# Re-staging a fused sliding-window attention and SwiGLU kernel: token pairs per partition, loads and casts one tile ahead, denominators by exp(-ln), one SiLU function

## The chip, the cores and the metric

The kernel runs on one core of one Trainium2 chip. The metric is the device time of one execution in microseconds (us), and a kernel is quoted by the median of its runs. An execution that is over 1.5% above the fastest of its kernel counts as slow and is left out of the ratios.

Engine names are those of the profile: PE is TensorE (matmul), PEld its weight load, DVE is VectorE, ACT is ScalarE, POOL is GpSimd and SP is SyncE. SPq, ACTq and POOLq are the sequencers of those engines, here mostly issuing DMA transfers. "L217" is line 217 of the kernel that was profiled.

## The reference

Attention over 8 batches, 8 heads, 576 positions and head size 64, in which each query sees only itself and the 63 positions before it; the result, 4608 tokens of width 512, goes through a SwiGLU block of width 1536.

```python
def _attn_ref(q, k, v):                       # [8, 8, 576, 64] each, float32
    scores = 1.0 / np.sqrt(64) * np.matmul(q, k.transpose(0, 1, 3, 2))
    rel = pos[:, None] - pos[None, :]
    mask = (rel >= 0) & (rel < 64)
    scores = np.where(mask, scores, -1e9)
    attn = softmax(scores)                     # [cut: written out in numpy]
    return np.matmul(attn, v)

def _moe_ref(x, w_gate, w_val, w_out):        # [4608, 512], [512, 1536] x2, [1536, 512]
    g = x @ w_gate
    silu = g * (1.0 / (1.0 + np.exp(-g)))
    val = x @ w_val
    return silu * val @ w_out
```

## The kernel before

The 4608 tokens are cut into nine tiles of 512. A tile's attention is done in four units, one for each pair of heads. A unit's parts are: load q, k and v; cast them to bf16 on GpSimd; transpose q and k on TensorE; copy k into a block-diagonal tile `kbd` (two heads share 128 rows); scores; exp; mask; products with v; and division by the row sum. The row sum comes from a matmul with a block of ones, so that it already stands in every row that needs it.

```python
    def transposes(u):                  # [cut: eight transposes into one PSUM tile tp]
        nc.scalar.copy(qT[:], tp[:, 0, :])
        kt = tp[:, 1, :].rearrange("r (j x) -> r j x", x=64)
        nc.vector.tensor_copy(kb[0:64, p, :, 0:64], kt[0:64])
        nc.vector.tensor_copy(kb[64:128, p, :, 64:128], kt[64:128])

    def scores(u):                      # [cut: per half, score matmuls into s_ps]
            nc.scalar.activation(Ef[...], s_ps[...], AF.Exp, scale=0.125)
            nc.gpsimd.tensor_mul(Ef[...], Ef[...], mask[...])

    def products(u):                    # [cut: E times v into o_ps]
        for c in range(2):
            nc.tensor.matmul(d_ps[:], bones[:], E[:, :, c, :], start=(c == 0), stop=(c == 1))
        r = att.tile([P, 512], FP32, name="r", tag="r")
        nc.vector.reciprocal(r[:], d_ps[:])
        nc.vector.tensor_mul(xT[t][:, p, :], o_ps[:], r[:])

    def gate_value(t, m):               # [cut: four gate and four value matmuls]
        nc.scalar.activation(th[:], g_ps[:], AF.Tanh, scale=0.5)
        nc.vector.scalar_tensor_tensor(sg[:], th[:], 1.0, g_ps[:], ALU.add, ALU.mult)
        nc.vector.tensor_mul(hT[t][:, m, :], sg[:], v_ps[:])
```

In the steady part each unit of attention is woven between three of the feed-forward block's twelve gate/value groups and one of the four output projections of the tile before:

```python
        gate_value(t, 3 * s)
        products(w + 4)
        gate_value(t, 3 * s + 1)
        transposes(w + 5)
        project(t - 1, s, ps_o, "o")
        load(w + 8)                     # up to 20 DMA issues on SyncE
        casts(w + 6)
        scores(w + 5)
        gate_value(t, 3 * s + 2)
```

Weights are loaded as float32 and cast by VectorE.

The softmax here doesn't subtract the row's maximum and nothing guards it: scores larger than these inputs give would overflow.

Of the kernel before, what the change touches and what calls it, by code (L numbers as in the profile page):

```python
# [17 lines left out]
def kernel(  # L18
# [10 lines left out]





# [4 lines left out]
    NU = NT * 4  # L38
# [3 lines left out]
    stage = ctx.enter_context(tc.tile_pool(name="stage", bufs=4))  # L42
    wst = ctx.enter_context(tc.tile_pool(name="wst", bufs=4))
    cast = ctx.enter_context(tc.tile_pool(name="cast", bufs=2))
    att = ctx.enter_context(tc.tile_pool(name="att", bufs=3))
    xpool = ctx.enter_context(tc.tile_pool(name="xpool", bufs=3))
    fsb = ctx.enter_context(tc.tile_pool(name="fsb", bufs=3))
    hpool = ctx.enter_context(tc.tile_pool(name="hpool", bufs=2))
    ps_a = ctx.enter_context(tc.tile_pool(name="ps_a", bufs=3, space=PSUM))
    ps_f = ctx.enter_context(tc.tile_pool(name="ps_f", bufs=2, space=PSUM))  # L50
    ps_o = ctx.enter_context(tc.tile_pool(name="ps_o", bufs=1, space=PSUM))
# [5 lines left out]
    vbd = [cst.tile([P, 4, 8, P], BF16, name=f"vbd{i}") for i in range(2)]  # L57
    identb = cst.tile([P, P], BF16, name="identb")
    bones = cst.tile([P, P], BF16, name="bones")
    mask = cst.tile([P, 8, 2, 64], BF16, name="mask")  # L60
# [13 lines left out]
    def load(u):  # L74
        t, p = divmod(u, 4)
        q_f = stage.tile([P, 4, 2, D], FP32, name="q_f", tag="q_f")
        k_f = stage.tile([P, 4, 2, D], FP32, name="k_f", tag="k_f")
        v_f = stage.tile([P, 8, D], FP32, name="v_f", tag="v_f")
        for dst, src in ((q_f, q), (k_f, k)):
            for off, b, s0, n in segments(t):  # L80
                o, s, left = off, s0, n
                while left:
                    if o % P or left < P:
                        m, r = 64, 64
                    else:
                        m, r = left // P * P, P
                    for a in range(2):
                        nc.sync.dma_start(  # L88
                            dst[o % P:o % P + r, o // P:o // P + max(1, m // P), a, :],
                            src[b, 2 * p + a, s:s + m].rearrange("(c r) d -> r c d", r=r),  # L90
                        )
                    o, s, left = o + m, s + m, left - m
        for off, b, s0, n in segments(t):
            for a in range(2):
                nc.sync.dma_start(
                    v_f[64 * a:64 * a + 64, off // 64:(off + n) // 64],
                    v[b, 2 * p + a, s0:s0 + n].rearrange("(j r) d -> r j d", r=64),
                )
        staged[u] = (q_f, k_f, v_f)
# [3 lines left out]
    def casts(u):  # L103
        t, p = divmod(u, 4)
        q_f, k_f, v_f = staged.pop(u)
        q_b = cast.tile([P, 4, P], BF16, name="q_b", tag="q_b")
        k_b = cast.tile([P, 4, P], BF16, name="k_b", tag="k_b")
        nc.gpsimd.tensor_copy(q_b[:], q_f[:].rearrange("r c h d -> r c (h d)"))  # L108
        nc.gpsimd.tensor_copy(k_b[:], k_f[:].rearrange("r c h d -> r c (h d)"))  # L109
        vb = vbd[t % 2]  # L110
        nc.gpsimd.tensor_copy(vb[0:64, p, :, 0:64], v_f[0:64])
        nc.gpsimd.tensor_copy(vb[64:128, p, :, 64:128], v_f[64:128])
        ready[u] = (q_b, k_b)

    raw = {}

    def weights_gv(s):
        for i, src in enumerate((moe_w_gate, moe_w_val)):
            w_f = wst.tile([P, 4, 384], FP32, name="w_f", tag="w_f")
            nc.sync.dma_start(  # L120
                w_f[:], src[:, 384 * s:384 * s + 384].rearrange("(c r) f -> r c f", r=P)
            )
            raw[i, s] = w_f

    def casts_gv(s):
        for i, dst in enumerate((wg, wv)):
            nc.vector.tensor_copy(dst[:, :, 384 * s:384 * s + 384], raw.pop((i, s))[:])

    def weights_o(s):
        w_f = wst.tile([P, 3, DM], FP32, name="wo_f", tag="w_f")  # L130
        nc.sync.dma_start(
            w_f[:], moe_w_out[384 * s:384 * s + 384].rearrange("(c r) f -> r c f", r=P)
        )
        raw[2, s] = w_f

    def casts_o(s):
        nc.vector.tensor_scalar_mul(wo[:, 3 * s:3 * s + 3, :], raw.pop((2, s))[:], 0.5)
# [3 lines left out]
    def transposes(u):  # L141
        t, p = divmod(u, 4)
        q_b, k_b = ready.pop(u)
        tp = ps_a.tile([P, 2, 512], BF16, name="tp", tag="a")
        for i, x in enumerate((q_b, k_b)):
            for c in range(4):
                nc.tensor.transpose(tp[:, i, P * c:P * c + P], x[:, c, :], identb[:])  # L147
        qT = att.tile([P, 512], BF16, name="qT", tag="qT")
        nc.scalar.copy(qT[:], tp[:, 0, :])  # L149
        kb = kbd[t % 2]  # L150
        kt = tp[:, 1, :].rearrange("r (j x) -> r j x", x=64)
        nc.vector.tensor_copy(kb[0:64, p, :, 0:64], kt[0:64])  # L152
        nc.vector.tensor_copy(kb[64:128, p, :, 64:128], kt[64:128])  # L153
        queries[u] = qT
# [3 lines left out]
    def scores(u):  # L158
        t, p = divmod(u, 4)
        qT = queries.pop(u)  # L160
        E = att.tile([P, 8, 2, 64], BF16, name="E", tag="E")
        Ef = E[:].rearrange("r m c x -> r (m c x)")
        for h in range(2):
            s_ps = ps_a.tile([P, 512], FP32, name="s_ps", tag="a")
            lo = 0
            if u < 4 and h == 0:
                lo = 64
            else:
                j = 4 * h - 1
                kb = kbd[t % 2][:, p, j, :] if j > 0 else kbd[(t - 1) % 2][:, p, 7, :]  # L170
                nc.tensor.matmul(s_ps[:, 0:64], kb, qT[:, 256 * h:256 * h + 64])
            for i in range(4):
# [4 lines left out]
                    kbd[t % 2][:, p, j, :],  # L177
# [5 lines left out]
            nc.gpsimd.tensor_mul(  # L183
                Ef[:, 512 * h + lo:512 * h + 512],
                Ef[:, 512 * h + lo:512 * h + 512],
                mask[:].rearrange("r m c x -> r (m c x)")[:, lo:512],
            )
            if t < 8 and t // 4 == h:
                nc.gpsimd.memset(E[:, t, 0, :], 0.0)
        weights[u] = E  # L190

    xT = {}

    def products(u):
        t, p = divmod(u, 4)
        E = weights.pop(u)
        Ef = E[:].rearrange("r m c x -> r (m c x)")
        if p == 0:
            xT[t] = xpool.tile([P, 4, 512], BF16, name="xT", tag="xT")
        o_ps = ps_a.tile([P, 512], FP32, name="ao_ps", tag="a")  # L200
        first = True
        for j in range(-1, 8):
            if j < 0 and t == 0:
                continue
            vb = vbd[t % 2][:, p, j, :] if j >= 0 else vbd[(t - 1) % 2][:, p, 7, :]
# [7 lines left out]
        d_ps = ps_a.tile([P, 512], FP32, name="ad_ps", tag="a")  # L213
        for c in range(2):
            nc.tensor.matmul(d_ps[:], bones[:], E[:, :, c, :], start=(c == 0), stop=(c == 1))  # L215
        r = att.tile([P, 512], FP32, name="r", tag="r")
        nc.vector.reciprocal(r[:], d_ps[:])  # L217
        nc.vector.tensor_mul(xT[t][:, p, :], o_ps[:], r[:])  # L218
# [3 lines left out]
    def gate_value(t, m):  # L222
# [10 lines left out]
        th = fsb.tile([P, 512], FP32, name="th", tag="th")  # L233
        nc.scalar.activation(th[:], g_ps[:], AF.Tanh, scale=0.5)  # L234
        sg = fsb.tile([P, 512], FP32, name="sg", tag="sg")
        nc.vector.scalar_tensor_tensor(sg[:], th[:], 1.0, g_ps[:], ALU.add, ALU.mult)  # L236
        nc.vector.tensor_mul(hT[t][:, m, :], sg[:], v_ps[:])  # L237

    def project(t, s, pool, tag):
# [132 lines left out]
```

## Time and profile before

| | before |
|---|---|
| time, median of 3 runs | 470.83 us (470.55 to 471.91) |
| span in the profile | 468.9 us |
| TensorE busy | 367.7 us, 78% of the span |
| VectorE busy | 338.8 us, 72% |
| RECIPROCAL | 36 x 3353 ns = 120.7 us |
| period of a steady unit | 11.53 us (46.14 us for a tile of four) |

The next fence has lines of the profile's page of the kernel before. The first gives each engine's busy time, share of the span and number of instructions. The next two give the chain that ended last, as shares of the span, by engine and by line. The last is a group of instructions: output and inputs, shapes, count, then busy us and mean ns of one, then the idle time of the engine just before them and what ended it.

```profile
PE 367.7 (78%) x2332; PEld 189.3 (40%) x2332; DVE 338.8 (72%) x380; ACT 145.2 (31%) x253; POOL 176.9 (38%) x258
...
DVE 52%; PE 35%; ACT 4%; SPq 3%; issue 2%; POOL 2%; DMA 1%; DVEq 0%; POOLq 0%; ACTq 0%
DVE r L217 24%; PE g_ps L229 14%; PE v_ps L229 9%; DVE hT L237 9%; DVE sg L236 8%; PE o_ps L242 6%; DVE xT L218 5%; PE s_ps L175 4%; ACT th L234 3%; SPq L88 2%; POOL E L183 2%; DVE kbd_93 L153 1%; DVE kbd_94 L153 1%; DVE kbd_93 L152 1%; PE ad_ps L215 1%
...
L217 DVE RECIPROCAL r<-ad_ps 128x512 f32<-128x512 f32 x36 | 120.7, 3353 | 5.0 <-PE ad_ps L215 5.0
```

The busy shares of the first line suggest that TensorE is the engine to watch. The chain says otherwise: 52% of the chain is VectorE, and RECIPROCAL alone is 24% of the span. A chain reads better than a busy share where two engines take turns waiting for each other. Here is one unit of the steady part from the same kernel's chain of waits, one piece a line: start in us, length in us, what it was (the other matmul groups and VectorE's last hT are left out).

```profile
210.62 3.28 DVE r L217
...
213.92 0.69 DVE xT L218
214.61 0.60 DVE sg L236
...
215.31 0.69 DVE hT L237
216.00 0.33 DVE kbd_93 L152
...
216.34 0.44 DVE kbd_93 L153
...
216.82 0.37 PE s_ps L175 x4
...
217.42 0.86 PE g_ps L229 x4
...
220.04 0.61 ACT th L234
...
220.67 0.70 DVE sg L236
...
222.15 3.28 DVE r L217
```

TensorE's own timeline has one marked wait in this unit. The columns are start, length, engine, line, operation, operands and count, and in brackets the idle time before it and what ended it:

```profile
216.82 0.37 PE L175 MATMUL s_ps<-qT,kbd_93 128*128 128x128 bf16 x4 [1.81 <-DVE kbd_93 L153]
```

From one RECIPROCAL to the next is 222.15 - 210.62 = 11.53 us. The chain goes from the row sum's RECIPROCAL (3.28) to its multiply, then to VectorE's waiting work for the gate groups (sg and hT), then to the two kbd copies, then to the scores that need kbd, then to the gate groups that stand behind the scores on TensorE, and from their Tanh and multiplies back to VectorE. A unit's matmuls, issued back to back, take only 9.5 us in this timeline: 5.19 for six gate/value groups, 2.59 for a projection, 0.44 for transposes, 0.44 for scores, 0.45 for products and 0.43 for denominators.

Before the steady part, which begins at 102 us, the first gate matmul stands at 40.8 us.

### The profile page before, as it was taken

What the parts mean: (1) busy time and instruction counts of PE and PEld (TensorE: products, weight loads), DVE (VectorE), ACT (ScalarE), POOL (GpSimd) and SP (SyncE); (2) the same over time, 40 slices, a digit from 0 to 9 for tenths busy, and PEclk for the clock granted to TensorE, in tenths of its full rate; (3) what the DMA queues carried; (4) which work ended last, traced back from release to release, by engine and by line L of the source; (5) the groups of instructions that cost most, each with busy time, mean ns of one, the idle gap of its engine ahead of it and who ended that gap; (6) DMA issues with size and microseconds to landing.
All of it is one profiled execution on the core that took longest, in us unless ns stands there. A gap on an engine that the chain in (4) does not pass through costs nothing.

```text
span 468.9 us, 6826 instructions
## 1 busy us (share of the span) xinstructions
PE 367.7 (78%) x2332; PEld 189.3 (40%) x2332; DVE 338.8 (72%) x380; ACT 145.2 (31%) x253; POOL 176.9 (38%) x258
## 2 busy tenths in 40 slices
PE   1453866738888888888888888888888888889996
PEld 0331433414444444444444444444444444444443
DVE  7188798777777777777777777777777777776540
ACT  1220222313333333333333333333333333323232
POOL 3873445424444444444444444444444433110000
PEclk9975897879999999999999999999999999999999
DMA  7965567741332355333333443233343330001012
GB/s 173 253 182 130 154 183 209 219 104 46 87 87 67 79 138 124 87 76 82 87 86 92 119 111 90 70 90 92 90 113 92 91 89 24 22 24 45 22 46 89
DMA packets 129314, 47.65 MB, mean 102 GB/s; under 512 B 119040, under 2 KB 123136, under 8 KB 129280
## 3 DMA queue, kind: packets, MB, share of 16 engines
q1 hardware_dynamic: 129280, 47.22, 39.3%
q8 instruction: 18, 0.29, 0.3%
q14 instruction: 16, 0.13, 0.1%
HBM read 37.75 MB, written 9.44 MB: 101 GB/s over the span
## 4 chain that ended last, share of the span: by engine, by line
DVE 52%; PE 35%; ACT 4%; SPq 3%; issue 2%; POOL 2%; DMA 1%; DVEq 0%; POOLq 0%; ACTq 0%
DVE r L217 24%; PE g_ps L229 14%; PE v_ps L229 9%; DVE hT L237 9%; DVE sg L236 8%; PE o_ps L242 6%; DVE xT L218 5%; PE s_ps L175 4%; ACT th L234 3%; SPq L88 2%; POOL E L183 2%; DVE kbd_93 L153 1%; DVE kbd_94 L153 1%; DVE kbd_93 L152 1%; PE ad_ps L215 1%
## 5 line engine op out<-in xcount | busy, mean ns | idle before, releaser
L183 POOL TENSOR_TENSOR E<-E,mask 128x512 bf16<-128x512 bf16 (+1 forms) x72 | 84.5, 1185 | 215.4 <-ACT E L180 215.4
L236 DVE SCALAR_TENSOR_TENSOR sg<-th,g_ps 128x512 f32<-128x512 f32 x108 | 73.9, 684 | 86.5 <-ACT th L234 86.4
L217 DVE RECIPROCAL r<-ad_ps 128x512 f32<-128x512 f32 x36 | 120.7, 3353 | 5.0 <-PE ad_ps L215 5.0
L229 PE MATMUL g_ps<-xT,wg 128*128 128x512 bf16 x432 | 115.4, 391 | 2.9 <-DVE xT L218 2.9
L229 PE MATMUL v_ps<-xT,wv 128*128 128x512 bf16 x432 | 114.3, 388 | 0.0
L234 ACT ACTIVATE th<-g_ps 128x512 f32<-128x512 f32 x108 | 64.5, 597 | 128.4 <-PE g_ps L229 128.4
L242 PE MATMUL o_ps<-wo,hT 128*128 128x512 bf16 x432 | 98.6, 379 | 0.0
L237 DVE TENSOR_TENSOR hT<-sg,v_ps 128x512 bf16<-128x512 f32 x108 | 74.2, 687 | 11.6 <-PE v_ps L229 0.6
L229 PEld LDWEIGHTS <-wv 128*128 128x128 bf16 x432 | 43.3, 100 | 57.2 <-issue 8.6
L180 ACT ACTIVATE E<-s_ps 128x512 bf16<-128x512 f32 (+1 forms) x72 | 39.1, 592 | 68.6 <-PE s_ps L175 68.6
L242 PEld LDWEIGHTS <-hT 128*128 128x128 bf16 x432 | 41.1, 98 | 44.6
L229 PEld LDWEIGHTS <-wg 128*128 128x128 bf16 x432 | 40.9, 100 | 44.5 <-issue 3.5
L175 PE MATMUL s_ps<-qT,kbd_93 128*128 128x128 bf16 (+1 forms) x160 | 14.0, 232 | 33.0 <-DVE kbd_93 L153 31.6
L149 ACT COPY qT<-tp 128x512 bf16<-128x512 bf16 x36 | 21.1, 586 | 45.6 <-PE tp L147 45.6
L175 PE MATMUL s_ps<-qT,kbd_94 128*128 128x128 bf16 (+1 forms) x128 | 10.3, 224 | 29.2 <-DVE kbd_94 L153 29.2
L147 PE MATMUL tp<-identb,q_b 128*128 128x128 bf16 x144 | 14.8, 229 | 16.9 <-POOL q_b L108 16.9
L215 PE MATMUL ad_ps<-E,bones 128*128 128x512 bf16 x72 | 23.1, 405 | 5.4 <-DVE r L217 5.4
L175 PEld LDWEIGHTS <-kbd_93 128*128 128x128 bf16 x160 | 10.8, 107 | 39.1 <-DVE kbd_93 L153 36.3
L218 DVE TENSOR_TENSOR xT<-ao_ps,r 128x512 bf16<-128x512 f32 x36 | 24.9, 692 | 1.2
L108 POOL CAST q_b<-q_f 128x512 bf16<-128x512 f32 x36 | 22.7, 630 | 6.1 <-DMA q_f<-in_q_dram 4.5
L109 POOL CAST k_b<-k_f 128x512 bf16<-128x512 f32 x36 | 22.1, 613 | 4.3 <-PE g_ps L229 3.3
L147 PEld LDWEIGHTS <-q_b 128*128 128x128 bf16 x144 | 11.3, 102 | 26.0 <-POOL q_b L108 18.2
(77 smaller groups left out, 240.7 us busy)
## 6 DMA issues: line engine op xcount, KB each, us to landing
w_f<-in_moe_w_gate_dram SPq DMA_DIRECT2D x4, 768.0 KB, 5.4
w_f<-in_moe_w_val_dram SPq DMA_DIRECT2D x4, 768.0 KB, 7.1
q_f<-in_q_dram SPq DMA_DIRECT2D x32, 96.0 KB, 3.8
k_f<-in_k_dram SPq DMA_DIRECT2D x32, 96.0 KB, 2.4
wo_f<-in_moe_w_out_dram SPq DMA_DIRECT2D x4, 768.0 KB, 6.0
q_f<-in_q_dram SPq DMA_DIRECT2D x16, 128.0 KB, 2.8
k_f<-in_k_dram SPq DMA_DIRECT2D x16, 128.0 KB, 3.2
v_f<-in_v_dram SPq DMA_DIRECT2D x16, 128.0 KB, 3.2
```

The lines of the kernel that those rows point to most:

```text
L147: nc.tensor.transpose(tp[:, i, P * c:P * c + P], x[:, c, :], identb[:])
L175: nc.tensor.matmul(s_ps[:, 64 + P * i:64 + P * i + n], kbd[t % 2][:, p, j, :], qT[:, 64 * j:64 * j + n],)
L180: nc.scalar.activation(Ef[:, 512 * h + lo:512 * h + 512], s_ps[:, lo:512], AF.Exp, scale=0.125)
L183: nc.gpsimd.tensor_mul(Ef[:, 512 * h + lo:512 * h + 512], Ef[:, 512 * h + lo:512 * h + 512], mask[:].rearrange("r m c x -> r (m c x)")[:, ...
L215: nc.tensor.matmul(d_ps[:], bones[:], E[:, :, c, :], start=(c == 0), stop=(c == 1))
L217: nc.vector.reciprocal(r[:], d_ps[:])
L218: nc.vector.tensor_mul(xT[t][:, p, :], o_ps[:], r[:])
L229: nc.tensor.matmul(ps[:], w[:, c, P * m:P * m + P], xT[t][:, c, :], start=(c == 0), stop=(c == 3),)
L234: nc.scalar.activation(th[:], g_ps[:], AF.Tanh, scale=0.5)
L236: nc.vector.scalar_tensor_tensor(sg[:], th[:], 1.0, g_ps[:], ALU.add, ALU.mult)
L237: nc.vector.tensor_mul(hT[t][:, m, :], sg[:], v_ps[:])
L242: nc.tensor.matmul(o_ps[:], hT[t][:, c, P * s:P * s + P], wo[:, c, :], start=(c == 0), stop=(c == 11),)
```

## The change

The intent is to take VectorE off the chain, so that TensorE alone sets the pace. The parts:

- **Staging by whole tiles.** A partition holds two adjacent tokens of all eight heads. From the third tile on, q and k come in a few large transfers; during a tile's gates those of the tile after next are cast and transposed, and the scores of the next tile stand in the same stretch as this tile's products. Even and odd tokens are put back into order by the copies to `kbd` and `xT`, which write every second element.
- **Denominators.** GpSimd adds the two halves of E first (F), so that one matmul is enough; and 1/d is made as exp(-ln d) by ScalarE.
- **SiLU.** One Silu on ScalarE replaces Tanh and a VectorE instruction. Two table sets are now needed, and the kernel switches between them by hand, twice a tile.
- **Weights** are cast by the DMA, issued from GpSimd. Output copies go from ScalarE to VectorE.
- **The first two tiles** are written apart: loads by head on SyncE and ScalarE, k casts and masks on VectorE, and the buffers of the second tile zeroed only after the first tile's attention.

The diff, cut to its core:

```diff
-    def casts(u):                      # per unit, on GpSimd; now per tile:
+    def cast_qk(t):
+        casts(t)
+        for g in range(2):
+            for e in range(2):
+                for i in range(2):
+                    cast_unit(nc.gpsimd, t, i, g, e=e)
[cut]
-        nc.vector.tensor_copy(kb[0:64, p, :, 0:64], kt[0:64])
-        nc.vector.tensor_copy(kb[64:128, p, :, 64:128], kt[64:128])
+        kt = tp[:, 1, :].rearrange("r (j e x) -> r j e x", j=8, e=2)
+        for a in range(2):
+            r = slice(64 * a, 64 * a + 64)
+            kb = kbd[t % 2][r, u, :, r].rearrange("r j (x e) -> r j e x", e=2)
+            nc.vector.tensor_copy(kb, kt[r])
[cut]
+        nc.gpsimd.tensor_add(F[:], E[:, :, 0, :], E[:, :, 1, :])
[cut]
-        for c in range(2):
-            nc.tensor.matmul(d_ps[:], bones[:], E[:, :, c, :], start=(c == 0), stop=(c == 1))
-        nc.vector.reciprocal(r[:], d_ps[:])
+        nc.tensor.matmul(d_ps[:], bones[:], F[:].rearrange("r m x -> r (m x)"))
+        nc.scalar.activation(ld[:], d_ps[:], AF.Ln)
+        nc.scalar.activation(r[:], ld[:], AF.Exp, scale=-1.0)
[cut]
-        nc.scalar.activation(th[:], g_ps[:], AF.Tanh, scale=0.5)
-        nc.vector.scalar_tensor_tensor(sg[:], th[:], 1.0, g_ps[:], ALU.add, ALU.mult)
+        nc.scalar.activation(sg[:], g_ps[:], AF.Silu)
[cut]
+    loads_by_head(0, nc.sync, nc.scalar)
+    set_exp()
+    loads_by_head(1, nc.sync, nc.sync)
[cut]
+    attention(0, lambda: weights_gv(0, 384))
+    set_silu()
+    nc.vector.memset(kbd[1][:], 0.0)
+    nc.vector.memset(vbd[1][:], 0.0)
+    nc.vector.memset(vbd[2][:], 0.0)
+    for m in range(3):
+        gate_value(0, m)
+    set_exp()
+    attention(1, rest)                 # rest(): the other eight weight loads, on GpSimd
[cut: the other gates of tiles 0 and 1]
+    for u in range(4):
+        transposes(2, u)
+        if u == 0:
+            project(0, 0)
+        scores(2, u)
+        cast_v(2, u)
+        masks(2, u, nc.vector)
+        if u:
+            project(0, u)
+    cast_qk(3)
+    loads_qk(4)
+    for u in range(4):
+        transposes(3, u)
+        products(2, u)
+        project(1, u)
+        scores(3, u)
+    set_silu()
+    for t in range(2, NT):             # the steady part [cut: `if`s that end it at the last tile]
+        if t > 2:                      # [cut: loads_qk(t + 2), loads_v(t + 1)]
+            set_exp()
+            for u in range(4):
+                products(t, u)
+                if u % 2 == 0:
+                    project(t - 1, u // 2)
+            for u in range(4):
+                scores(t + 1, u)
+                if u % 2 == 1:
+                    project(t - 1, 2 + u // 2)
+            set_silu()
+        cast_qk(t + 2)
+        for m in range(12):
+            gate_value(t, m)
+            if m % 3 == 2:
+                u = m // 3
+                cast_v(t + 1, u)
+                masks(t + 1, u)
+                transposes(t + 2, u)
```

## The prediction

> **What bounds the kernel now.** In the chain of waits of the steady part, a unit (a quarter of a 512-token tile) repeats every 11.54 us: RECIPROCAL 3.28, its multiply 0.69, sg/hT of the blocked gate blocks, kbd copies 0.33+0.44, then scores, gates, and the next RECIPROCAL. So VectorE paces the units (RECIPROCAL: 24% of the chain, 120.7 us busy), TensorE being 85% busy. From the TensorE timeline, a unit's matmuls issued back to back take: six gate/value groups of 0.86 = 5.19, project 2.59, transposes 0.44, scores 0.44, products 0.45, denominators 0.43: 9.5 us. The last four units, without attention, take 7.77, all TensorE. Before the steady part (from 102 us) TensorE is mostly idle or at a low clock: first gates at 40.8 us, halted until 45 for the fourth xT; then RECIPROCALs, VectorE weight casts and GpSimd masks alternate on the chain.
>
> **What changes.** VectorE loses 36 RECIPROCALs (120.7), 108 STTs (73.9), weight casts (15.6); it gains 36 output copies (about 0.69 each, 25) and the first tiles' masks and k casts; kbd copies may slow, writing every second element. ScalarE: th (0.60) becomes Silu, same size; 72 Ln/Exp of about 0.6 are added, output copies removed, and 18 table loads added. The Trainium skill, "ScalarE: Activation LUTs", What ACT_TABLE_LOAD costs, gives about 1283 ns a load; this trace's one load took 1.28. TensorE loses one 512-column matmul per unit (0.215). GpSimd per steady tile: 8 casts of 0.62, 8 v casts of 0.61, 8 masks and 4 adds of 1.19, about 25 us, below a tile's time.
>
> **The new bound: TensorE.** Per tile 4 x (9.5 - 0.215) = 37.2 us against 46.1; VectorE about 18-20, ScalarE about 24. Where products, projections and next scores alternate, PSUM slots chain Ln 0.6, Exp 0.6, multiply 0.7 before a score matmul: about 1 us of stall, so 38-39 us a tile.
>
> Sum (estimate from trace durations):
> - First tile: unit-sized DMAs on two queues, first transpose near 5 us; units paced at about 5.5 us by cast - transpose - scores - exp - mask - add; first gates near 30 us instead of 41-45.
> - Second tile's attention after three gates has little matmul work to hide it: another 25-28 us. From about 65 us on TensorE is fed continuously. The second tile's per-head loads are 64 issues at about 0.55 us on one queue, done near 42 us, in time.
> - Matmul work left then: 9 x 37.2 - (two attentions 12.4, three gates 5.2) = 318 us.
> - Stalls: 7 steady tiles x 1.2 = 9; tiles 2 and 3, where scores directly follow their transposes, 7; cold clock 2.
> - Tail: copy 0.7, store about 2, and the 2 us between span and time: 5.
>
> Total 406; I predict **405 us, 80% range 395 to 419**. Chances: faster by over 2% 0.97, within 2% 0.02, slower 0.01.
>
> **What would show it.** Right: TensorE about 95% or more busy from about 65-70 us to the end; chain mostly gate, value and project matmuls; tile period 38-39 us; table loads of 1.28 us on ScalarE but nearly absent from the chain; small idle at score matmuls waiting for xT or exp. Wrong: first gates later than 35 us or continuous feeding later than 72 us (weight DMAs from GpSimd, adds behind them); period of 41 us or more with score matmuls waiting on r/xT, Silu waits behind table loads, or GpSimd masks and casts late for products or transposes.
>
> **What would make it wrong.** GpSimd held off by VectorE's two-input masks and casts in the first tiles; slow weight DMAs with cast; strided kbd or xT writes much slower than 0.7 us; the table loads draining ScalarE longer than their 1.28 us; TensorE's clock falling in the second attention and staying low.

## The result, and the profile after

The changed kernel is correct. Ratios here and below are the mean time of one kernel's fast runs over the mean time of the other's fast runs in the same rounds, so they are not quite the ratio of the medians quoted beside them.

| | before | after |
|---|---|---|
| time, median | 471.37 us (470.55 to 471.93, 4 runs) | 415.25 us (413.19 to 420.56, 4 runs) |
| ratio of fast runs | | 0.8801 (0.8775 to 0.8827) |
| span in the profile | 468.9 us | 413.7 us |
| TensorE busy | 367.7 us, 78% | 359.3 us, 87% |
| VectorE busy | 338.8 us, 72% | 200.5 us, 48% |
| period of a steady tile | 46.14 us | 38.25 us |
| first gate matmul | 40.8 us | 35.1 us |
| gates of the third tile begin | 148.05 us | 153.4 us |

One of the four runs after, 420.56 us, is 1.8% above the fastest, so it counts as slow and is not in the ratio. Its mean granted clock, 0.946, is hardly below the 0.949 of the fastest run, so what made it slow isn't shown.

From the page of the changed kernel, the lines that answer to those of before (engines' busy time; the chain by engine; one group):

```profile
PE 359.3 (87%) x2296; PEld 189.2 (46%) x2296; DVE 200.5 (48%) x300; ACT 187.5 (45%) x306; POOL 190.3 (46%) x281
...
PE 77%; SPq 7%; DMA 7%; ACT 2%; POOL 2%; DVE 2%; issue 2%; ACTq 0%; POOLq 0%
...
L170 DVE COPY kbd<-tp 64x512 bf16<-64x512 bf16 x72 | 52.2, 725 | 35.6 <-ACT qT L165 35.1
```

The chain is now 77% TensorE, where it was 35%. The table load, which was feared, does not show among the large parts. The kbd copies have got slower: 725 ns on average for 64x512 elements, against 406 and 427 ns for the two copies in the kernel before. They now write every second element, but no run separates that from the rest of the new layout.

The 7% each of SPq and DMA lie before 60.2 us: followed back, the chain of the start is load issues and landings. Whether the loads set the time of the start isn't settled by that: b4 leaves them alone and still brings the start forward by 7.7 us.

In the steady part the chain of waits of the changed kernel is nearly all matmul. This piece of it has the only wait that comes back in every steady tile:

```profile
218.94 2.59 PE o_ps L268 x12
...
222.67 0.21 PE s_ps L191 x4
...
222.95 0.59 ACT E L196
...
223.58 0.19 PE s_ps L187
```

Three score matmul groups find free PSUM tiles; the fourth must wait until the first group's exp has freed one, and the chain steps to ScalarE for 0.59 us. In ScalarE's timeline that exp stands behind the Ln and Exp of the tile's last unit, which take it from 221.78 to 223.04 us. The wait at that matmul, summed up by the view of waits for TensorE, comes 5 times and takes 3.5 us in all, so 0.7 us a tile. Five steady periods are 38.24 to 38.25 us, so without that wait about 37.5, where the prediction estimated 37.2 of matmul work.

The start is another matter. These are lines of the changed kernel's TensorE timeline, with the columns of the TensorE line shown for the kernel before.

```profile
15.50 0.61 PE L158 MATMUL tp<-identb,k_b 128*128 128x128 bf16 x4 [6.71 <-DVE k_b L120]
...
20.77 0.74 PE L158 MATMUL tp<-identb,q_b 128*128 128x128 bf16 x4 [3.87 <-POOL q_b L120]
...
43.53 1.86 PE L257 MATMUL v_ps<-xT,wv 128*128 128x512 bf16 x4 [2.92 <-DVE hT L263]
...
69.80 0.59 PE L224 MATMUL ad_ps<-F,bones 128*128 128x512 bf16 x1 [4.74 <-POOL F L213]
...
72.37 1.82 PE L257 MATMUL g_ps<-xT,wg 128*128 128x512 bf16 x4
...
114.89 0.19 PE L187 MATMUL s_ps<-qT,kbd 128*128 128x64 bf16 x1 [1.04 <-ACT qT L165]
116.39 0.37 PE L191 MATMUL s_ps<-qT,kbd 128*128 128x128 bf16 x4 [1.31 <-DVE kbd L170]
```

Each bracket is a wait for an engine that is off the critical path in the steady part, but not here. The first line waits for a k cast on VectorE; the second for a q cast on GpSimd; the third for VectorE's hT; the fourth for F, which GpSimd makes; the last two for the copies of q and of k out of a transposed tile. The line at 72.37 is where TensorE is fed without long gaps from then on. Below, "the feed" means that moment, read the same way in each kernel's TensorE timeline.

The waits for q casts on GpSimd are the largest group in the start, 19.2 us in six waits (3.87, 2.55, 3.85 and 2.47 us among them). Each of these casts stands behind the F of the unit before in GpSimd's order (here F starts at 19.12 and the cast at 20.33 us), so that addition is a link in the pace of these units; b4 tests it.

How much of the gain is pace and how much is start? From the third tile's first gate matmul to the end the kernel of before takes 468.9 - 148.05 = 320.9 us and that of after 413.7 - 153.4 = 260.3 us. At that mark the changed kernel has done more: the second tile's four projections (4 x 2.59) and the transposes and scores of three further units (3 x 0.88), about 13 us of matmul work. So of the 55 us, an estimate from these numbers is about 47.6 us from the pace (60.6 - 13) and 7.7 us from the start (13 - 5.35).

### The profile page after: what moved, and what is told of

The parts are those of the page before. It is cut to its first block, busy times and chain, and to the rows that moved or that the text cites. A ratio compares the mean times of both kernels' runs of the same rounds, so it can differ in the third digit from the quotient of the medians.

```text
span 413.7 us, 6332 instructions
## 1 busy us (share of the span) xinstructions
PE 359.3 (87%) x2296; PEld 189.2 (46%) x2296; DVE 200.5 (48%) x300; ACT 187.5 (45%) x306; POOL 190.3 (46%) x281
## 2 busy tenths in 40 slices
DMA packets 88415, 42.89 MB, mean 104 GB/s; under 512 B 41280, under 2 KB 83776, under 8 KB 88384
## 4 chain that ended last, share of the span: by engine, by line
PE 77%; SPq 7%; DMA 7%; ACT 2%; POOL 2%; DVE 2%; issue 2%; ACTq 0%; POOLq 0%
PE g_ps L257 22%; PE v_ps L257 22%; PE o_ps L268 21%; DMA k_f<-in_k_dram 4%; PE ao_ps L233 4%; SPq L91 4%; PE tp L158 3%; PE s_ps L191 3%; SPq L101 2%; PE ad_ps L224 2%; DVE kbd L170 2%; DMA q_f<-in_q_dram 2%; ACT E L196 1%; DMA v_f<-in_v_dram 1%; SPq L86 1%
## 5 line engine op out<-in xcount | busy, mean ns | idle before, releaser
L262 ACT ACTIVATE sg<-g_ps 128x512 f32<-128x512 f32 x108 | 64.4, 597 | 105.3 <-PE g_ps L257 105.2
L209 POOL TENSOR_TENSOR E<-E,mask 128x512 bf16<-128x512 bf16 x48 | 54.3, 1152 | 35.0 <-ACT E L196 33.4
L170 DVE COPY kbd<-tp 64x512 bf16<-64x512 bf16 x72 | 52.2, 725 | 35.6 <-ACT qT L165 35.1
L268 PEld LDWEIGHTS <-hT 128*128 128x128 bf16 x432 | 40.8, 99 | 45.3 <-issue 2.8
L213 POOL TENSOR_TENSOR F<-E 128x512 bf16<-128x512 bf16 x36 | 41.6, 1156 | 16.6 <-DVE E L209 14.5
L118 POOL CAST q_b<-q_f 128x512 bf16<-128x512 f32 x28 | 17.2, 613 | 46.1 <-PE tp L158 46.1
L158 PE MATMUL tp<-identb,q_b 128*128 128x128 bf16 x144 | 17.2, 238 | 21.1 <-POOL q_b L120 19.2
L211 POOL MEMSET E<- 128x64 bf16 x32 | 4.8, 150 | 56.5 <-DVE E L209 55.3
L233 PEld LDWEIGHTS <-vbd 128*128 128x128 bf16 x320 | 23.3, 108 | 14.6 <-issue 9.2
L239 ACT ACTIVATE ld<-ad_ps 128x512 f32<-128x512 f32 x36 | 21.6, 599 | 18.5 <-PE ad_ps L224 18.3
L191 PE MATMUL s_ps<-qT,kbd 128*128 128x128 bf16 (+1 forms) x288 | 23.9, 232 | 4.2 <-DVE kbd L170 4.1
L233 PE MATMUL ao_ps<-E,vbd 128*128 128x128 bf16 x320 | 25.6, 234 | 0.0
L191 PEld LDWEIGHTS <-kbd 128*128 128x128 bf16 x288 | 19.5, 108 | 13.1 <-DVE kbd L170 8.0
```

The lines of the kernel that those rows point to most:

```text
L158: nc.tensor.transpose(tv[:, i, g, e], x[:, g, e, 2 * u:2 * u + 2, :].rearrange("r h d -> r (h d)"), identb[:],)
L170: nc.vector.tensor_copy(kb, kt[r])
L191: nc.tensor.matmul(s_ps[:, 64 + P * i:64 + P * i + n], kbd[t % 2][:, u, j, :], qT[:, 64 * j:64 * j + n],)
L209: eng.tensor_mul(part, part, mf[:, lo:512])
L213: nc.gpsimd.tensor_add(F[:], E[:, :, 0, :], E[:, :, 1, :])
L233: nc.tensor.matmul(o_ps[:, lo:hi], vb, Ef[:, e0:e0 + hi - lo], start=first, stop=(j == 7), skip_group_check=True,)
```

## The experiments

Except for b1, whose diff is against the kernel before, each diff is against the changed kernel; those of c2 and c3 show what they add to c1 and c2. All ratios are to the kernel before in the same rounds; the changed kernel's own is 0.8801.

The first four runs each move one thing in the start of the changed kernel, to test the reading of its TensorE timeline.

### a1: the zeroing of the second tile's buffers moved ahead

```diff
+            if t == 0 and u == 0:      # in attention(), behind the first casts
+                nc.vector.memset(kbd[1][:], 0.0)
+                nc.vector.memset(vbd[1][:], 0.0)
+                nc.vector.memset(vbd[2][:], 0.0)
[cut]
     set_silu()
-    nc.vector.memset(kbd[1][:], 0.0)
-    nc.vector.memset(vbd[1][:], 0.0)
-    nc.vector.memset(vbd[2][:], 0.0)
```

> The changed kernel, with the three VectorE memsets of 1.76 us (second kbd, second and third vbd) moved from before the first gates to the first unit, where VectorE sat idle from 6.2 to 13.7 us. Theory (the 10 us above the prediction are work queued in the wrong order on one in-order engine): the 2.9 us halt of the value matmul at 40.6-43.5 us goes, the v casts on GpSimd no longer wait 6.3 us, TensorE is fed continuously from about 68.5 instead of 72.4 us, time about 411 us against 415.2. Rival (the data of the second tile, whose last loads are issued at 48 us, sets the pace): the first gates lose their halt, but the continuous feed starts within 1 us of 72.4 and the time stays at 415.

Measured: 413.89 us (413.15 to 415.98), ratio 0.8798 (0.8764 to 0.8831). The wait of 2.92 us for hT at the value matmul is gone from TensorE's waits. The feed comes at 69.2 us, 3.2 us earlier, but the median is only 1.4 us lower, and the interval includes the ratio of the changed kernel. Of the 3.2 us the profiled pair keeps 2.3 (spans of 413.7 and 411.4 us), since the stretch from the feed to the third tile's gates takes 81.9 us instead of 81.0. First gates stand at 35.9 instead of 35.1; that is before the feed. So the memsets do stand where the reading put them, but no gain in time is clear of the noise.

### a2: the second batch of weight loads issued two units earlier

```diff
-            if u == 3:
+            if u == (3 if t == 0 else 1):
                 after()
```

> The changed kernel, with the eight weight DMAs of GpSimd issued after the v cast of the second unit of the second tile (GpSimd idle there from 44.2 to 52.8 us) instead of the fourth, where they hold GpSimd from 62.2 to 68.4 us ahead of two adds. Theory: the 4.7 us wait of the denominator matmul for F goes, feed from about 67.5 us, time about 410.5 us. Rival (transfers limit): the 7.7 MB of weights now run beside the second tile's loads, its fourth unit comes later, and the feed starts no earlier than 71 us.

These are lines of the changed kernel's GpSimd timeline that the run was aimed at:

```profile
62.20 0.78 POOL L140 DMA_DIRECT2D wg<-in_moe_w_gate_dram  x1
...
66.64 1.70 POOL L145 DMA_DIRECT2D wo<-in_moe_w_out_dram  x2
...
68.61 1.14 POOL L213 TENSOR_TENSOR F<-E 128x512 bf16<-128x512 bf16 x1
```

Eight DMA issues hold GpSimd from 62.20 to 68.38 us, about 0.77 us each, and the F of the last two units stands behind them: that is the 4.74 us wait of TensorE at 69.80.

Measured: 415.21 us (414.66 to 416.94), ratio 0.8817 (0.8791 to 0.8844). The longest wait for F fell from 4.7 to 1.4 us and the feed came at 68.3, 4.1 us earlier. The time did not move at all. The stretch from the feed to the third tile's gates grew from 81.0 to 84.6 us, with two of its projections at a low clock (4.1 and 4.68 us for twelve matmuls, where 2.75 is usual). An earlier feed is not worth its length if the stretch behind it then runs longer.

### a3: ScalarE issues no loads

```diff
-    loads_by_head(0, nc.sync, nc.scalar)
+    loads_by_head(0, nc.sync, nc.sync)
```

> The changed kernel, with all loads of the first tile issued by SyncE; none by ScalarE. Theory: ScalarE's 12 issues, which wait for earlier loads to land, hold its table load until 11.75 us and the first query copy until 13.05 us; freed, the copy runs near 6.5 us, first gates near 29 instead of 35.1 us, feed from about 67 us, time about 409 us. Rival (the loads themselves are late): units two to four wait for their casts' data instead, the first gates stay at 34-35 us, the time within 1.5 us of 415.2.

The two fences show ScalarE's timeline, first of the changed kernel (its last issue, then its first work):

```profile
11.12 0.60 ACTq L101 DMA_DIRECT2D v_f<-in_v_dram  x1
11.75 1.28 ACT L280 ACT_TABLE_LOAD   x1 [11.75 <-DMA v_f<-in_v_dram]
13.05 0.59 ACT L165 COPY qT<-tp 128x512 bf16<-128x512 bf16 x1
```

and then of this run:

```profile
0.80 1.28 ACT L280 ACT_TABLE_LOAD   x1 [0.80 <-PEq L437]
7.05 0.58 ACT L165 COPY qT<-tp 128x512 bf16<-128x512 bf16 x1 [4.97 <-PE tp L158]
```

The issues of ScalarE do not only cost their 0.6 us each. They are spread until 11.72 us, and the table load and the first copy of transposed q stand behind them in ScalarE's order, although the first unit's transposes were done at 6.6 us. With all loads on SyncE, the first copy comes at 7.05 instead of 13.05.

Measured: 410.54 us (408.92 to 413.43), ratio 0.8719 (0.8673 to 0.8764). First gates at 29.1 us, which is the 30 that had been predicted; the feed at 65.5, 6.9 us earlier; the median 4.7 us lower. The Trainium skill, "DMA: Bandwidth & Descriptors", section "Issuing engines are not separate DMA queues", says that issuing from several engines saves only the sequencer's time for issuing, because the transfers share the same DMA engines. This run agrees and adds that it can cost: here the second issuer cost about 4 us by the ratios (4.7 by the medians).

### a4: tiles two and three in another order

Tiles are counted from zero here and in the code: these are the third and fourth.

```diff
         transposes(2, u)
-        if u == 0:
-            project(0, 0)
-        scores(2, u)
         cast_v(2, u)
-        masks(2, u, nc.vector)
         if u:
-            project(0, u)
+            scores(2, u - 1)
+            masks(2, u - 1, nc.vector)
+        project(0, u)
[cut: in the second loop project(1, u) goes first, and scores(3, u - 1) follow products(2, u)]
```

> The changed kernel, where in tiles two and three a unit's scores follow the next unit's transposes and a projection of 2.59 us, instead of directly following their own transposes. Theory: of the 44.1 us from 109.4 to 153.5 us about 30.5 are matmuls at full clock; the rest is TensorE waiting for query copy 0.59 and key copies 1.46 before the scores, plus a lower clock after these waits (0.75 in 130-140 us). Expected 36 us for the stretch, clock 1.00, time about 407-408 us. Rival: the stretch is paced by GpSimd's casts of the third tile and by ScalarE, then it stays above 41 us and the time above 412.

Measured: 408.89 us (408.13 to 409.08), ratio 0.8674 (0.8654 to 0.8693), the largest gain of the four. The waits for the copies of q and k (1.04 and 1.31, then twice 0.67 and 1.30 in the changed kernel) are gone, because a projection of 2.59 us now stands between a unit's transposes and its scores. The stretch from the feed to the third tile's gates is 74.9 us instead of 81.0, and the time follows in full: 6.4 us.

The wait was long because the two copies do not overlap. In the changed kernel the first kbd copy of a unit starts 0.02 to 0.03 us after the q copy's end, and in 34 of the 36 units VectorE is listed as idle until then. The Trainium skill, "PSUM — Partial Sum Buffer", section "PSUM bank collisions raise a hardware error", says that two engines may not touch the same bank and partition quadrant at once, even if both read. The transposed q and k are two halves of one PSUM tile here, and a copy of q (0.59) and two of k (1.45) follow each other. The trace agrees with the page, but it doesn't show in which bank a tile lies, and a program that orders accesses by tile would look the same. c2 below gives each half a tile of its own.

The low clock of this stretch is seen in the changed kernel's windows. The columns are: start and end of the window, its length, then busy us and instruction count of each engine; the last three are the granted TensorE clock as a share of full speed, the DMA share and GB/s.

```profile
110.00:120.00 10.00, 7.50 (x61) 4.11 (x59) 6.05 (x11) 3.90 (x7) 4.06 (x7) 1.00 0.07 28
120.00:130.00 10.00, 6.05 (x45) 3.28 (x44) 5.58 (x10) 3.34 (x6) 3.46 (x7) 0.91 0.14 52
130.00:140.00 10.00, 8.13 (x39) 3.81 (x37) 2.87 (x4) 1.72 (x3) 5.60 (x9) 0.75 0.59 157
```

TensorE is busy 7.50 and 6.05 of 10 us in the first two windows, and in the third the granted clock is 0.75: the projections at 128.57 and 137.18 take 4.28 and 3.40 us. From 140 to 150 TensorE is busy throughout and the clock is full again. In a4 only one is slow (3.74).

### b1: the kernel before, with its RECIPROCAL replaced by a copy

This gives a wrong result (relative error 6.4 million); it asks what RECIPROCAL alone was worth in the old staging.

```diff
-        nc.vector.reciprocal(r[:], d_ps[:])
+        nc.vector.tensor_copy(r[:], d_ps[:])
```

> The kernel before, with RECIPROCAL replaced by a plain copy from PSUM of the same shape (about 0.69 instead of 3.35 us); the result is wrong on purpose. Theory (RECIPROCAL alone set the 11.54 us unit): VectorE's unit falls to about 8.9 us, TensorE's 9.5-9.8 takes over, 28 units save about 50 us and the start some 10, time about 405-412 us, as good as the changed kernel. Rival (the whole re-staging of the change was needed): the interleaved chain th - sg - hT - gates keeps units above 10.5 us, time above 430 us.

Measured: 426.70 us (425.17 to 427.93), ratio 0.9059 (0.9029 to 0.9090). It fell between what the two theories expected: 44 of the 56 us. Two windows of this run, columns as above:

```profile
190.00:250.00 60.00, 56.13 (x355) 28.49 (x354) 34.79 (x56) 20.96 (x40) 27.83 (x40) 0.95 0.36 88
250.00:400.00 150.00, 150.00 (x963) 77.44 (x962) 92.64 (x150) 57.69 (x104) 57.79 (x81) 1.00 0.35 89
```

From 250 to 400 us TensorE is busy in all of 150 us, and a unit takes 9.55 us. So RECIPROCAL was what held the old steady unit at 11.53. But from 190 to 250 TensorE stands idle for 3.9 us at a clock of 0.95, and there the chain of waits of this run shows another limit:

```profile
238.41 0.63 SPq L95
...
239.08 0.62 SPq L95
...
239.75 3.48 DMA v_f<-in_v_dram
```

Ahead of these lines the chain is SyncE's load issues, one after another, from 229 us on. In these units a unit has 20 loads (8 of q, 8 of k, 4 of v), which take about 12 us to issue, more than the 9.55 us of matmul work. Between 144 and 164 us casts on GpSimd wait for loads too. At the pace of RECIPROCAL this did not show. The new staging removes this limit as well: a tile is loaded in some 22 issues rather than in up to 80.

### b2: the changed kernel, with RECIPROCAL put back

```diff
-        nc.scalar.activation(ld[:], d_ps[:], AF.Ln)
-        nc.scalar.activation(r[:], ld[:], AF.Exp, scale=-1.0)
+        nc.vector.reciprocal(r[:], d_ps[:])
```

> The changed kernel, with Ln and Exp on ScalarE replaced by the VectorE RECIPROCAL of before; all else as changed. VectorE then has about 33 us of work in a tile of 38 us, but 19 us of it in the 15 us stretch of products and projections. Theory: this stretch and the first tiles' chain grow, tile period 41-42 us, time 430-445 us. Rival (VectorE had room enough once the other work left it): within 2% of 415.

Measured: 487.01 us (484.38 to 489.73), ratio 1.0342 (1.0287 to 1.0397), slower than the kernel before, and far worse than the 430 to 445 that had been expected. Four pieces of its chain of waits say why:

```profile
249.84 3.37 DVE r L239
...
254.60 3.28 DVE r L239
...
258.68 3.25 DVE r L239
...
262.80 0.21 PE s_ps L187
```

The new order puts four products close together, so four RECIPROCALs stand in a row on VectorE. Each holds its PSUM tile for over 3 us, and TensorE's score matmuls wait for one to come free (2.63 us at 261.98, then 0.24 at 262.80, the line shown). A steady tile takes 46.5 us (45.3 to 48.2), as long as before, and the feed comes at 84.2 us instead of 72.4. The expectation had only counted VectorE's time. So this staging needs the RECIPROCAL gone. The reverse, exp(-ln) in the old staging, was not run; b1 stands in for it, with a cheaper copy and a wrong result. Nor was RECIPROCAL in a staging that spreads the products apart.

### b3: the changed kernel, with Tanh and two VectorE instructions for SiLU

```diff
-        nc.scalar.activation(sg[:], g_ps[:], AF.Silu)
-        nc.vector.tensor_mul(hT[t][:, m, :], sg[:], v_ps[:])
+        nc.scalar.activation(th[:], g_ps[:], AF.Tanh, scale=0.5)
+        nc.vector.scalar_tensor_tensor(th[:], th[:], 1.0, g_ps[:], ALU.add, ALU.mult)
+        nc.vector.scalar_tensor_tensor(
+            hT[t][:, m, :], th[:], 0.5, v_ps[:], ALU.mult, ALU.mult
+        )
```

The table set `exp_and_others` takes the place of the SiLU set, so the number of table loads stays the same.

> The changed kernel, with Silu replaced by Tanh and two VectorE operations (a factor 0.5 in the second); table loads stay 18. VectorE gains 0.69 us per gate block, 8.2 us a tile. Theory (the one-function SiLU is off the critical path, TensorE is the limit): period at most 39 us, time 415-420 us. Rival: VectorE's work in the gate stretch (12 x 1.38 plus 5.8 us of key copies in 22.5 us) becomes the limit, time above 425 us.

Measured: 420.26 us (419.42 to 423.24), ratio 0.8935 (0.8900 to 0.8971), 5 us slower. The steady tile is unchanged at 38.23 to 38.24 us in four of five periods (38.70 in the first): with TensorE as the bound, VectorE's extra 0.68 us for each of 108 groups costs nothing there. Of the 3.9 us between the two profiled spans (417.6 and 413.7), 3.3 lie between the feed and the third tile's gates (84.3 us against 81.0). That stretch varies from 80.8 to 84.6 among variants which leave it alone. The loss is clear, since the two intervals don't overlap, but whether SiLU itself or a shifted moment of low clock makes it stays open.

### b4: the changed kernel, with two denominator matmuls and no pre-addition

```diff
-        F = epool.tile([P, 8, 64], BF16, name="F", tag="F")
-        nc.gpsimd.tensor_add(F[:], E[:, :, 0, :], E[:, :, 1, :])
-        nc.tensor.matmul(d_ps[:], bones[:], F[:].rearrange("r m x -> r (m x)"))
+        for c in range(2):
+            nc.tensor.matmul(d_ps[:], bones[:], E[:, :, c, :], start=(c == 0), stop=(c == 1))
```

> The changed kernel without the pre-add: two 512-column denominator matmuls accumulate again, the 36 GpSimd adds of 1.15 us go. Theory: each steady tile grows by 4 x 0.215 = 0.86 us (38.25 to 39.1), 6 us over the seven tiles, while the first two tiles, where the add is a link of the unit's chain (5.85 us a unit), get about 1 us a unit faster; time 414-419 us. Rival (the pre-add is worth its matmuls in full): 423 us, with no earlier start.

Measured: 412.04 us (409.67 to 415.13), ratio 0.8753 (0.8705 to 0.8802): a median 3 us lower, but the two intervals overlap, so whether the change is better without this part isn't settled. A steady tile takes 39.06 us, 0.8 longer, which is what four matmuls of 0.215 us cost. But the feed comes at 64.7, 7.7 us earlier. Where TensorE is the bound, the pre-addition saves what it promised; in the first two tiles, where a unit waits for its own chain, GpSimd's addition of 1.16 us is one more link of that chain: a unit there takes about 4.6 us without it and 5.85 with it.

### c1: a1, a2, a3 and a4 together

> All four re-orderings at once on the changed kernel: memsets early, weight DMAs issued earlier, first tile's loads all issued by SyncE, scores of tiles two and three behind a projection. Theory (they remove separate waits, and where a single one gave back what it saved, as with the early weights, it was the low clock after the waits of tiles two and three): feed from 58-60 us instead of 72.4, tiles two and three 37 us, time 393-398 us. Rival (behind them lies one common limit, the landing of the second tile's loads): feed no earlier than 63 us, time above 401 us.

Measured: 406.53 us (405.79 to 407.00), ratio 0.8635 (0.8622 to 0.8647), against the 393 to 398 of the theory that the gains add. The feed came at 71.5 us, hardly earlier than in the changed kernel: a3's 6.9 us were gone. GpSimd's timeline in this run names the reason:

```profile
63.35 0.61 POOL L135 CAST vbd<-v_f 64x512 bf16<-64x512 f32 x1 [5.66 <-DMA v_f<-in_v_dram]
66.38 0.61 POOL L136 CAST vbd<-v_f 64x512 bf16<-64x512 f32 x1 [2.43 <-DMA v_f<-in_v_dram]
```

The v casts of the second tile's last unit wait 5.66 and 2.43 us for loads. The rival was right: behind the order of work stands the arrival of the second tile's data. It needs 64 issues of about 0.47 us each on SyncE, and its transfers share the DMA engines with the weights, most of which now start earlier. The traces point at those weights: the last unit's 16 issues take from 42.5 to 57.0 us here, right behind eight weight loads issued from 38.4 to 44.5. In a3, with the same 64 issues but the weights from 55.3 us, they take from 43.8 to 52.5, its v casts there wait at most 0.21 us, and its feed comes six us earlier than here, at 65.5. That speaks against the number of issues alone; c1 without a2 was not run.

### c2: c1, with a PSUM bank for each half of the transposed tile and two denominator matmuls in the first two tiles

```diff
+        if t < 2:
+            tq = ps_a.tile([P, 512], BF16, name="tp", tag="a")
+            tk = ps_f.tile([P, 512], BF16, name="tk", tag="v")
[cut: q is transposed into tq, k into tk; F is made only for t >= 2]
```

> As the run with all four re-orderings, and in the first two tiles only: the transposed queries and keys in two PSUM banks, so that VectorE's key copies need not wait for ScalarE's query copy (0.59 us a unit), and two denominator matmuls instead of the GpSimd add (1.15 us a unit). Theory: units of the first two tiles are a chain of small operations, so each shortens by 1.2-1.7 us; feed 6-9 us earlier than with the four re-orderings alone, time 386-391 us. Rival (loads): feed at most 3 us earlier.

Measured: 407.54 us (405.92 to 408.28), ratio 0.8663 (0.8648 to 0.8677), no better than c1. The kbd copies of the first two tiles no longer wait for the q copy: TensorE's transpose of k is now named as what released them. So the serial order came with the shared tile. Since each half has both a tile and a bank of its own now, the run can't tell the bank from the program's tracking of the tile. The feed is at 69.8 us all the same: TensorE waits up to 8.0 us for a q cast, and GpSimd waited for loads before it. Shortening a unit's chain is worth nothing while its data are not there.

### d1: q and k of the third tile and later in pieces half as long

```diff
-                    eng.dma_start(
-                        dst[p0:p0 + r, g].rearrange("r h e d -> r h (e d)"),
-                        src[b, :, s:s + m].rearrange("h (r e) d -> r h (e d)", e=2),
-                    )
+                    for e in range(2):
+                        eng.dma_start(
+                            dst[p0:p0 + r, g, :, e, :],
+                            src[b, :, s:s + m].rearrange("h (r e) d -> r h e d", e=2)[:, :, e, :],
+                        )
```

> The changed kernel, with the query and key loads from the third tile on split by token parity: 256 B instead of 512 B pieces and twice the issues, all else the same. Theory (loads of these tiles run a tile ahead, off the critical path): DMA share of 0.45 in the steady tiles grows towards 0.6, time within 2 us of 415.2. Rival (the paired layout earns part of the gain through its transfers): time above 419 us, with casts waiting for loads.

Measured: 416.72 us (415.90 to 418.17), ratio 0.8856 (0.8834 to 0.8878), 0.6% above the changed kernel. The packets rise from 88415 to 117696, the steady tile stays at 38.2 us, and the DMA share rises only from 0.39 to 0.42, where 0.6 was expected. The pairing of tokens in a partition doubles the length of a contiguous piece, but in the steady part that length is off the critical path. The 0.6% is clear, since the intervals don't overlap, but the profiled spans are alike (414.0 and 413.7 us), so where it arises isn't shown.

### c3: the second tile's loads in 22 issues instead of 64

This run takes c2 and changes three things more: q and k of the second tile come as whole-tile loads, as they do for later tiles; the first weight loads are issued one unit earlier and the rest behind the last v cast again, as in the changed kernel; and two denominator matmuls are used in the first three tiles, where VectorE, which does the masks there, also zeroes the column block that the mask doesn't reach.

```diff
     set_exp()
-    loads_by_head(1, nc.sync, nc.sync)
+    loads_qk(1)
+    loads_v(1)
[cut]
-            if u == (3 if t == 0 else 1):
+            if u == (2 if t == 0 else 3):
                 after()
[cut]
-            nc.gpsimd.memset(E[:, t, 0, :], 0.0)
+            eng.memset(E[:, t, 0, :], 0.0)
-        if t >= 2:
+        if t >= 3:
```

> The run with the four re-orderings and the two short-cuts in the first tiles, with three differences: the second tile's loads are issued as 22 DMAs (6 of whole rows of heads) instead of 64 by head; the weight DMAs go back behind the second tile's last v cast, the first pair one unit earlier; the first three tiles use two denominator matmuls and VectorE zeroes the masked block, so GpSimd holds nothing that products wait for. Theory (what was left at the start was the landing of the second tile's loads, 64 issues of about 0.5 us and then shared with 7.7 MB of weights): no wait of casts for loads above 1 us in the second tile, feed from 52-57 us instead of 70-72, tiles two and three about 35.5 us, time 386-394 us. Rival (the first two tiles' chain itself or the weights bind): feed after 62 us or gates waiting for weights, time above 399 us.

Measured: 384.92 us (384.52 to 386.88), ratio 0.8173 (0.8139 to 0.8206), correct, and the fastest kernel: 30.3 us below the changed kernel, and better than the 386 to 394 expected. Its windows, columns as above:

```profile
28.40:53.30 24.90, 17.37 (x143) 11.01 (x141) 16.92 (x36) 15.83 (x26) 15.43 (x26) 0.79 0.88 167
53.30:90.90 37.60, 36.70 (x175) 16.59 (x173) 15.01 (x22) 15.02 (x25) 7.84 (x14) 1.00 1.11 193
90.90:123.70 32.80, 31.98 (x286) 19.27 (x284) 24.52 (x41) 17.19 (x32) 7.68 (x13) 1.00 0.49 141
123.70:350.00 226.30, 222.77 (x1474) 116.58 (x1472) 112.32 (x161) 121.55 (x197) 132.65 (x176) 1.00 0.35 88
```

The first line is the second tile's attention together with the first three gate groups: the feed comes at 53.3 us instead of 72.4. From then on TensorE is busy in 36.70 of 37.60, 31.98 of 32.80 and 222.77 of 226.30 us, at full clock. In the sum of its waits nothing is left but the casts of the first two tiles, the 0.7 us of each steady tile and single waits below 1 us; no group of matmuls after the feed ran at a low clock. The mean granted clock is 0.987, against 0.955 in the changed kernel.

One part of the expectation was wrong: the first q casts of the second tile still waited 5.48 and 1.90 us for their load. The waits ended by 28.06 us, before TensorE had a use for them. The three differences to c2 were not run apart, so how the 22.6 us between c2 and c3 divide among fewer issues, later weights and VectorE's zeroing is open.

## Why the prediction was right, and where its sum was off

**The bound.** "VectorE paces the units", by way of RECIPROCAL: shown. b1 takes RECIPROCAL out of the old kernel, and its unit falls from 11.53 to 9.55 us, the estimated matmul work of 9.5, with TensorE busy in all of 150 us.

**The new bound.** "38-39 us a tile", TensorE: shown. Five steady periods are 38.24 to 38.25 us, with one wait of 0.7 us a tile; b3 and d1 add VectorE and DMA work without moving it, and b4 adds 0.86 us of matmul work and moves it by 0.8. The prediction named the wait as scores behind "Ln 0.6, Exp 0.6, multiply 0.7"; it is scores behind Ln, Exp and then an exp of earlier scores, without the multiply. Its size, "about 1 us", was nearly right.

**The table loads.** "nearly absent from the chain": right. There are 18 of 1283 ns, and one of them is on the chain, at 109 us, between the first two tiles' gates and the third tile's transposes.

**The sum.** The time was 415.2, not 405: inside the range, though two of the prediction's own marks of being wrong were narrowly met, first gates at 35.1 (35) and the feed at 72.4 (72), the second for the reason that it names, weight DMAs from GpSimd with adds behind them. The terms show where:

| term | predicted | measured |
|---|---|---|
| first gates | 30 us | 35.1 us |
| first gates to the feed | 35 us | 37.3 us |
| stalls of tiles two and three, with the cold clock | 7 + 2 us | about 13.5 us |
| stalls of the steady tiles | 9 us | about 5 us |
| feed to the end | 341 us | about 343 us |

The last line agrees within 2 us partly by luck: the two terms of stalls above it, which it contains, were some 4 us too small and 4 too large.

The step that failed most is "First tile: unit-sized DMAs on two queues, first transpose near 5 us ... first gates near 30 us". The first transpose did come at 5.01 us, and from the second unit's k transposes on (15.50, 21.31, 27.16) a unit takes about 5.85 us, near the 5.5 predicted. What was left out is that the second queue is ScalarE's, so ScalarE could do no work until 11.72 us. a3 shows it: without ScalarE's issues the first gates come at 29.1 us.

"Second tile's attention ... another 25-28 us" and "done near 42 us, in time" had the loads right as far as this kernel's order asked for them; the extra came from memsets (2.92 us of wait, a1) and weight issues on GpSimd (4.74 us, a2). The issues had been named as a risk but given no size. That the loads are in fact close behind was shown only once the rest was taken away: c1 and c2 stall on them, and c3, with a third of the issues and the weights moved back, does not; the two were not run apart.

For "tiles 2 and 3, where scores directly follow their transposes, 7", the mechanism was right and the size was off. The waits for copies add up to 6.3 us (1.04 + 1.31 + 2 x (0.67 + 1.30)); casts of the fourth tile add 1.8, and a slowed clock stretched two projections by 1.53 and 0.65 us; the remaining 3 us or so of the 13.5 are smaller waits and slowed small matmuls, which were not itemised. That the copies are serial, and that the k copies need 725 ns each, had both been missed. a4 removes the waits and gains 6.4 us.

**What the parts are worth.** The gain is not a sum of parts. Taking RECIPROCAL off VectorE is what frees the pace; the new staging alone, with RECIPROCAL, loses 3.4% to the kernel before (b2), and the old staging without RECIPROCAL, which could not be right in its result, gains 9.4% (b1) and then meets SyncE's issues. The pre-addition costs about as much in the start as it saves later, or more (b4), and what Silu is worth, none of it in the steady part, stays open (b3).

## What to carry to other kernels

When a change moves the bound to TensorE, the pace is then easy to predict from the matmul work, and the error sits in the start: for every engine that is to work early, write down all it has been given to do in program order before that, DMA issues and memsets among it. A part that pays where the matmul engine is the bound can cost where a chain is (the pre-addition, 0.8 us won on each steady tile and, in one pair of profiles, 7.7 us lost before), so choose per stage. And gains in a start do not add: after a few are taken, find what arrives last, here the second tile's loads, and ask what holds it up: their 64 issues or the weights beside them, which no run here separates.

## What the Trainium skill lacked or had wrong

- "ScalarE: Activation LUTs", section "What ACT_TABLE_LOAD costs", gives about 1283 ns for a load, which all 18 loads here agree with, and about 1380 ns for a drain on top. No drain shows here. In ScalarE's timeline of the changed kernel the load starts 0.01 us after the activation before it has ended, and the next begins 0.02 us after the load:

```profile
35.15 0.63 ACT L241 ACTIVATE r<-ld 128x512 f32<-128x512 f32 x1
35.79 1.28 ACT L283 ACT_TABLE_LOAD   x1
37.09 0.60 ACT L262 ACTIVATE sg<-g_ps 128x512 f32<-128x512 f32 x1
```

- "TensorE: Matmul & The Clock Gate", section "HAM oscillation — how this bites in real kernels", has the rule that TensorE should not be idle for over about 3.4 us at a time. In the changed kernel the granted clock fell to 0.75 between 130 and 140 us after gaps of at most 1.31 us each, in windows in which TensorE was busy 75% and 61% of the time. The page describes frequent short gaps as a further cause, in "A second HAM failure mode: psum-queue depth-cycling", but gives no busy share below which it happens.
- "VectorE: DVE Perf Modes" explains that Reciprocal is an iterative divide with a repeat count, but gives no time. Here it takes 3353 ns for 128x512 elements, 4.8 times a multiply of that shape (692 ns).
- No page gives the time that GpSimd is held by issuing one DMA with a cast: 0.75 to 0.79 us for each gate and value load here (0.94 for the first), during which its additions wait.
